# Decoding float64 weights in wider chunks, with the multiply on VectorE instead of GpSimd

## The chip, the cores and the metric

The kernel runs on one core of a Trainium2 chip. The metric is the device time of one execution in microseconds (us). TensorE (PE) does the matmuls, and PEld is its loading of weights; VectorE (DVE), ScalarE (ACT) and GpSimd (POOL) work on tiles in SBUF; SyncE (SP) issues most of the transfers. Each engine takes its own instructions strictly in the order in which the program gives them, and waits where an operand isn't ready or a buffer isn't free.

## The reference

Sigmoid attention is followed by an FFN with GELU. q, k and v are 8 x 12 x 448 x 64 (batches, heads, tokens, head size); the FFN has 3584 tokens, width 768 and hidden width 2048.

```python
scores = scale * np.matmul(q, k.transpose(0, 1, 3, 2)) - np.log(S)
attn = 1.0 / (1.0 + np.exp(-scores))
x = np.matmul(attn, v)          # heads side by side: 3584 x 768
h = x @ w_in                    # 768 x 2048
g = 0.5 * h * (1.0 + erf(h * inv_sqrt2))
out = g @ w_out                 # 2048 x 768
```

q, k and v are float32. The two weight matrices come in as float64, and the kernel gets them as 64-bit integers.

## The kernel before

**Splitting.** Matmuls run on float32 values in a rounded format, fp32r. Where more bits are wanted a value is split in two: ACT casts it to fp32r (the high part) and DVE subtracts that from the value (the low part). So `prepare_to` makes of every weight unit a tile `whl` with both parts (L236 on ACT, L237 on DVE), and `split_head` does the same for q and k of a head: `qs` (L291, L292) and `ka`, `kb` (cast L294, subtractions of 64 and 384 columns, L295 and L299).

**Decoding.** A chunk is 128 partitions by up to 384 weights, each with a low and a high 32-bit word. `start` takes the exponent bits `e` out of the high word with a mask (L124), shifts the mantissa `m` into place (L125) and joins bits of the low word to it (L128), all on DVE. `convert` makes a float32 power of two of `e` with two activations on ACT (L136, L139) and turns `m` from a signed integer into a float from 1 to 2 (L141 on DVE; for chunks 24 to 39 L145 on ACT). `end` joins the sign to `e` on DVE (L153), and GpSimd multiplies `m` by `e` (L162). The three steps are a pipeline: one step of the decoder runs `start` of chunk i, `convert` of chunk i-1 and `end` of chunk i-2, and then issues raw loads ahead of need on SP's queue (`load_to`, up to 8 raw buffers for the first 40 chunks). There are 32 chunks of `w_in` (16 units of 768) and 36 of `w_out` (12 units of 1024). A decoded unit is used from SBUF in the first pass over the tokens and stored to DRAM (L200) for the six passes after it.

**Order.** The order of all work is written out by hand. `attention_first` does the attention of batches 0 and 1, 24 heads one after the other. Per head `scores` does eight matmuls, the sigmoids on ACT and `split_head` for the head after the next; after every second head `values` does 16 matmuls for the pair, a cast on ACT (`xh`) and a subtraction on DVE (`xl`). Between `scores` and `values` stands `W.decode(n)`, which runs the decoder up to step n; PACE_A sets how many steps fall into this stage, PACE_F how many into `ffn1` of the first pass. Score and value tiles share four PSUM buffers, tag `pav`; the other score tile (`sc`, two key blocks) has one buffer.

Then come seven passes t of 512 token columns: `ffn1(t)`, 16 blocks of 18 matmuls with GELU behind each, and `window(t + 2, t)`, in which the 288 matmuls of `ffn2(t)` are cut into 24 parts and laid between the heads of the attention of batch t + 2. The last window has no attention left. Batches below 3 are "plain": their attention weights aren't split. In the first pass decoding goes on: one or two steps after each block of `ffn1`, three per head in `window`, until all chunks are done. In the first pass `prepare_to` in `ffn1` and `ffn2` splits a unit one or two units ahead of its matmuls, into two buffers `whl`.

Of the kernel before, what the change touches and what calls it, by code (L numbers as in the profile page):

```python
# [3 lines left out]

# [18 lines left out]
def tile_sigmoid_attention_gelu_ffn(  # L23
# [48 lines left out]


    PLAIN = 3
    RING = 3
    PACE_A, PACE_F = 20, 23
    SUB = 384
    RAW = (("raw", RING), ("a", 2)), (("raw", RING), ("a", 2), ("ah", 3))
    EARLY, AHEAD = PACE_A + PACE_F - 3, 4
    WST = 3  # L80
    SHIFT, KEPT = 1, 4
    AHD = 3
    MLO, MHI = 24, 40
# [7 lines left out]
    def decoder():  # L91


        chunks = [
            (kind, u, c0, min(SUB, width(kind) - c0))
            for kind, u in UNITS
            for c0 in range(0, width(kind), SUB)
        ]
        raws, parts, ended = {}, {}, [0]
        raw_ring = sb.tile([P, RING, 2 * SUB], U32, tag="raw", name="raw_ring", bufs=1)  # L100
        raw_next = itertools.cycle(range(RING))
        me_ring = sb.tile([P, RING, 2, SUB], U32, tag="me", name="me_ring", bufs=1)
        rings = [
            itertools.cycle([tag for n in range(4) for tag in ring if n < tag[1]]) for ring in RAW
        ]

        def load_to(n):
            for i in range(len(raws) + ended[0], min(n, len(chunks))):
                kind, u, c0, w = chunks[i]
                src = (w_in if kind == "in" else w_out)[u].rearrange("p a b -> p (a b)")  # L110
                tag, bufs = next(rings[i < EARLY])
                if tag == "raw":
                    raw = raw_ring[:, next(raw_next)]
                else:
                    raw = sb.tile([P, 2 * SUB], U32, tag=tag, name=f"raw{i}", bufs=bufs)
                raw = raw[:, : 2 * w]
                nc.sync.dma_start(raw.bitcast(I64), src[:, c0 : c0 + w])
                raws[i] = raw.rearrange("p (n t) -> p n t", t=2)

        def start(i):  # L120
            w = chunks[i][3]
            low, high = raws[i][:, :, 0], raws[i][:, :, 1]
            m, e = me_ring[:, i % RING, 0, :w], me_ring[:, i % RING, 1, :w]
            nc.vector.tensor_scalar(e, high, 0x7FF00000, None, op0=ALU.bitwise_and)  # L124
# [3 lines left out]
            nc.vector.scalar_tensor_tensor(  # L128
                m, low, 20, m, op0=ALU.logical_shift_right, op1=ALU.bitwise_or
            )  # L130
            parts[i] = m, e

        def convert(i):

            m, e = parts[i]
            nc.scalar.activation(  # L136
                e.bitcast(F32), e.bitcast(I32), AF.Relu, bias=1151.0 * 2**23, scale=-8.0
            )
            nc.scalar.activation(e, e.bitcast(F32), AF.Relu, bias=255.0 * 2**23, scale=-1.0)  # L139
            if not MLO <= i < MHI:  # L140
                nc.vector.tensor_scalar(  # L141
                    m.bitcast(F32), m.bitcast(I32), 2.0**-32, 1.5, op0=ALU.mult, op1=ALU.add
                )
            else:
                nc.scalar.activation(  # L145
                    m.bitcast(F32), m.bitcast(I32), AF.Identity, bias=1.5, scale=2.0**-32
                )

        def end(i):
            high = raws.pop(i)[:, :, 1]  # L150
            ended[0] += 1
# [10 lines left out]
            nc.gpsimd.tensor_tensor(t, m.bitcast(F32), e.bitcast(F32), op=ALU.mult)  # L162

        load_to(2)
        yield False
        for i in range(len(chunks) + 2):
            if i < len(chunks):
                start(i)
            if 0 <= i - 1 < len(chunks):
                convert(i - 1)  # L170
            if i > 1:
                end(i - 2)
            load_to(max(min(i + AHEAD + 1, EARLY), i + 2))
            yield i > 1 and chunks[i - 2][2] + chunks[i - 2][3] == width(chunks[i - 2][0])
# [109 lines left out]
    def split_head(b, h):  # L284
        b, h = there(b, h)
        if b >= B or h >= NH:
            return
        hp, j = divmod(h, 2)
        qr, kr = raws[b, hp]
        qs = sb.tile([P, S], F32R, tag="qs", name=f"qs{b}_{h}", bufs=3)  # L290
        nc.scalar.copy(qs[rows(j)], qr[rows(j)])  # L291
        nc.vector.tensor_tensor(qs[rows(1 - j)], qr[rows(j)], qs[rows(j)], op=ALU.subtract)  # L292
        ka = sb.tile([P, S + TAIL], F32R, tag="ka", name=f"ka{b}_{h}", bufs=3)
        nc.scalar.copy(ka[:, :S], kr[:, j])  # L294
        nc.vector.tensor_tensor(  # L295
            ka[:, S:], kr[:, j, S - TAIL :], ka[:, S - TAIL : S], op=ALU.subtract
        )
        kb = sb.tile([P, S - TAIL], F32R, tag="kb", name=f"kb{b}_{h}", bufs=3)
        nc.vector.tensor_tensor(  # L299
            kb, kr[:, j, : S - TAIL], ka[:, : S - TAIL], op=ALU.subtract  # L300
        )
        heads[b, h] = qs, ka, kb
        if j == 1 and b >= PLAIN:
            vr = raws[b, hp, "v"]
            vs = sb.tile([P, 2, 4, 2 * D], F32R, tag="vs", name=f"vs{b}_{hp}")
            nc.vector.tensor_copy(vs[:, :, :, :D], vr)
            nc.vector.tensor_tensor(vs[:, :, :, D:], vr, vs[:, :, :, :D], op=ALU.subtract)
            heads[b, hp, "v"] = vs

    def scores(b, h):  # L310
        plain = b < PLAIN
        qs, ka, kb = heads.pop((b, h))
        a = []
        for t in range(2):
            tag = ("al", ("wst", "wst", "ah")[b])[t] if plain else "a"
            bufs = {"wst": WST, "a": 2}.get(tag, 3)
            a.append(sb.tile([P, 2, S], F32, tag=tag, name=f"a{b}_{h}_{t}", bufs=bufs))
        last = ps_av.tile([P, 512], F32, tag="pav", name=f"sc{b}_{h}_l")[:, :S]
        sc0 = ps_av.tile([P, 512], F32, tag="pav", name=f"sc{b}_{h}_0")[:, :S]
        sc1 = ps_sc.tile([P, 2, 512], F32, tag="sc", name=f"sc{b}_{h}_1")[:, :, :S]  # L320
        if plain:
            nc.tensor.matmul(last[:D], ka[:, S - TAIL : S], qs, start=True, stop=False)
            nc.tensor.matmul(last[:D], ka[:, S:], qs, start=False, stop=True)
        else:

            nc.tensor.matmul(last, ka[:, S - TAIL :], qs, start=True, stop=True)  # L326
        for c in range(3):
            keys = slice(c * P, c * P + P)
            o = sc0 if c == 0 else sc1[:, c - 1]
            nc.tensor.matmul(o, ka[:, keys], qs, start=True, stop=False)  # L330
# [249 lines left out]
```

## Time and profile before

| | |
|---|---|
| median of 3 runs | 1288.09 us (1288.07 to 1288.74) |
| the profiled execution, its own time | 1286.42 us |
| its span, first to last instruction | 1284.7 us |
| PE busy | 1240.6 us (97%) |
| ACT busy | 872.5 us (68%) |
| DVE busy | 827.1 us (64%) |
| POOL busy | 89.2 us (7%) |

The profiled execution took 1.7 us longer than its span; the median of the runs is another 1.7 us higher. Matmuls are pipelined and their ends are modelled, so that the record of one lasts longer than the time by which it holds up the next: the distance of two starts is what PE needs. The same holds, by about 0.1 us, for neighbours on DVE and ACT. In a group line, the figures behind the bar are the busy time of the group in us and the mean duration of one instruction in ns, and behind the second bar the time for which the engine sat idle just before them, with what ended most of it. All of POOL's busy time lies in the first 300 us.

### The profile page before, as it was taken

What the parts mean: (1) busy time and instruction counts of PE and PEld (TensorE: products, weight loads), DVE (VectorE), ACT (ScalarE), POOL (GpSimd) and SP (SyncE); (2) the same over time, 40 slices, a digit from 0 to 9 for tenths busy, and PEclk for the clock granted to TensorE, in tenths of its full rate; (3) what the DMA queues carried; (4) which work ended last, traced back from release to release, by engine and by line L of the source; (5) the groups of instructions that cost most, each with busy time, mean ns of one, the idle gap of its engine ahead of it and who ended that gap; (6) DMA issues with size and microseconds to landing.
All of it is one profiled execution on the core that took longest, in us unless ns stands there. A gap on an engine that the chain in (4) does not pass through costs nothing.

```text
span 1284.7 us, 15676 instructions
## 1 busy us (share of the span) xinstructions
PE 1240.6 (97%) x5448; PEld 985.1 (77%) x5448; DVE 827.1 (64%) x1359; ACT 872.5 (68%) x1427; POOL 89.2 (7%) x84
## 2 busy tenths in 40 slices
PE   7888888999999999999999999999999999999998
PEld 4445665666888888888888888888888888888887
DVE  6776888883358873489734798436984358863420
ACT  8997777764459974499844898447995469964421
POOL 1112333440000000000000000000000000000000
PEclk9999998999999999999999999999999999999999
DMA  8664646652444314444234442244422444323331
GB/s 302 232 203 144 225 162 201 200 185 95 135 153 153 108 54 132 149 152 135 66 95 157 150 150 70 82 162 153 142 74 91 151 148 141 105 66 98 113 123 35
DMA packets 83775, 176.41 MB, mean 137 GB/s; under 512 B 24432, under 2 KB 37744, under 8 KB 83696
## 3 DMA queue, kind: packets, MB, share of 16 engines
q1 hardware_dynamic: 81968, 169.12, 40.6%
q0 software_dynamic: 1728, 6.29, 1.2%
q8 instruction: 43, 0.70, 0.2%
q14 instruction: 36, 0.29, 0.1%
HBM read 149.03 MB, written 26.35 MB: 137 GB/s over the span
## 4 chain that ended last, share of the span: by engine, by line
PE 82%; DVE 7%; ACT 5%; issue 2%; POOL 2%; DMA 2%; SPq 0%; DVEq 0%; POOLq 0%; ACTq 0%
PE po L496 11%; PE po L497 11%; PE po L498 11%; PE ph L449 11%; PE ph L451 11%; PE ph L450 11%; PE pav L397 7%; PE sc L330 4%; PE sc L331 4%; PE pav L363 2%; ACT a L354 2%; DVE whl L237 2%; POOL w_out L162 1%; DVE me_ring L153 1%; PE sc_l L326 1%
## 5 line engine op out<-in xcount | busy, mean ns | idle before, releaser
L449 PE MATMUL ph<-xh,whl 128*128 128x512 f32 x672 | 267.2, 398 | 10.6 <-DVE whl L237 10.6
L496 PE MATMUL po<-g,whl 128*128 128x512 f32 x672 | 264.1, 393 | 9.5 <-DVE whl L237 9.4
L450 PE MATMUL ph<-xl,whl 128*128 128x512 f32 x672 | 266.5, 397 | 0.0
L451 PE MATMUL ph<-xh,whl 128*128 128x512 f32 x672 | 266.3, 396 | 0.0
L497 PE MATMUL po<-g,whl 128*128 128x512 f32 x672 | 262.9, 391 | 0.0
L498 PE MATMUL po<-g,whl 128*128 128x512 f32 x672 | 262.8, 391 | 0.0
L237 DVE TENSOR_TENSOR whl<-wst,whl 128x768 fp32r<-128x768 f32 (+1 forms) x168 | 179.6, 1072 | 67.0 <-ACT whl L236 63.6
L466 DVE TENSOR_TENSOR g<-gf,g 128x512 fp32r<-128x512 f32 x112 | 77.8, 694 | 224.0 <-ACT g L465 224.0
L464 ACT ACTIVATE gf<-ph 128x512 f32<-128x512 f32 x112 | 66.9, 597 | 216.2 <-PE ph L451 201.5
L449 PEld LDWEIGHTS ph<-xh,whl 128*128 128x128 f32 x672 | 126.6, 188 | 44.7 <-DVE whl L237 13.7
L236 ACT CAST whl<-wst 128x768 fp32r<-128x768 f32 (+1 forms) x168 | 155.4, 928 | 2.2 <-PE po L498 0.8
L496 PEld LDWEIGHTS po<-g,whl 128*128 128x128 f32 x672 | 126.6, 188 | 39.0 <-DVE whl L237 11.8
L451 PEld LDWEIGHTS ph<-xh,whl 128*128 128x128 f32 x672 | 126.7, 188 | 30.7
L450 PEld LDWEIGHTS ph<-xl,whl 128*128 128x128 f32 x672 | 126.6, 188 | 30.3
L354 ACT ACTIVATE a<-sc 128x896 f32<-128x896 f32 x192 | 129.6, 727 | 27.8 <-PE sc L331 23.5
L498 PEld LDWEIGHTS po<-g,whl 128*128 128x128 f32 x672 | 126.6, 188 | 27.0
L497 PEld LDWEIGHTS po<-g,whl 128*128 128x128 f32 x672 | 126.6, 188 | 23.8
L330 PE MATMUL sc<-qs,ka 128*128 128x448 f32 x288 | 109.3, 379 | 13.2 <-ACT a L354 12.7
L347 DVE TENSOR_TENSOR al<-a,ah 128x896 fp32r<-128x896 f32 x120 | 97.8, 854 | 34.8 <-ACT ah L346 34.8
L331 PE MATMUL sc<-qs,kb 128*128 128x448 f32 x288 | 107.6, 374 | 0.0
L292 DVE TENSOR_TENSOR qs<-qr,qs 64x448 fp32r<-64x448 f32 x96 | 62.1, 646 | 45.1 <-ACT qs L291 43.3
L346 ACT CAST ah<-a 128x896 fp32r<-128x896 f32 x120 | 85.6, 753 | 6.1 <-PE pav L397 4.7
(62 smaller groups left out, 1514.1 us busy)
## 6 DMA issues: line engine op xcount, KB each, us to landing
wst<-scr_in SPq DMA_DIRECT2D x96, 384.0 KB, 3.0
wst<-scr_out SPq DMA_DIRECT2D x72, 512.0 KB, 3.2
kr<-k_dram SPq DMA_DIRECT2D x47, 448.0 KB, 4.5
vr<-v_dram SPq DMA_DIRECT2D x48, 256.0 KB, 4.1
qr<-q_dram SPq DMA_DIRECT2D x48, 224.0 KB, 3.2
out_dram<-ob SPq DMA_DIRECT2D x42, 224.0 KB, 2.0
raw<-w_in_dram SPq DMA_DIRECT2D x20, 384.0 KB, 4.6
scr_in<-w_in SPq DMA_DIRECT2D x16, 384.0 KB, 4.2
```

What stands on the lines that cost most here:

```text
L236: nc.scalar.copy(hl[:, 0, :w], t[:, :w])
L237: nc.vector.tensor_tensor(hl[:, 1, :w], t[:, :w], hl[:, 0, :w], op=ALU.subtract)
L330: nc.tensor.matmul(o, ka[:, keys], qs, start=True, stop=False)
L331: nc.tensor.matmul(o, kb[:, keys], qs, start=False, stop=True)
L347: nc.vector.tensor_tensor(al[t][:, c], a[t][:, c], ah[t][:, c], op=ALU.subtract)
L354: nc.scalar.activation(a, sc, AF.Sigmoid, bias=NEG_LOG_S, scale=SCALE)
L449: nc.tensor.matmul(ph, wl, xh[:, cc], start=cc == 0, stop=False)
L450: nc.tensor.matmul(ph, wh, xl[:, cc], start=False, stop=False)
L451: nc.tensor.matmul(ph, wh, xh[:, cc], start=False, stop=cc == NC - 1)
L496: nc.tensor.matmul(po, wl, g[fc][:, 0], start=first, stop=False)
L497: nc.tensor.matmul(po, wh, g[fc][:, 1], start=False, stop=False)
L498: nc.tensor.matmul(po, wh, g[fc][:, 0], start=False, stop=last)
```

## The change

Chunks are 768 wide for `w_in` and 512 for `w_out`: 16 and 24 of them instead of 32 and 36. The mantissa is kept as an unsigned integer with its leading one set (shift by 11, OR instead of XOR), so that conversion, scaling by 2^-31 and the product with `e` are one `scalar_tensor_tensor` on DVE. L141, L145 and the GpSimd multiply are gone; POOL still issues the stores of `w_out`. The decoder has two stages: a step runs `start` of chunk i, the two activations of the same chunk among it, and then `end` of chunk i-1. The raw words have three buffers, and chunk i+2 is loaded behind `end` of chunk i-1, whose buffer it takes. PACE_A and PACE_F are halved with the chunks; `window` has two steps per head instead of three, none directly behind `scores`.

In `split_head` the two k tiles become one, `ks`. For plain batches its low part is one subtraction of 448 columns, and for batches 0 and 1 the cast of k runs on DVE. `qs` and `ks` have two buffers instead of three. For batches from 3 on the two `a` tiles of a head are one tile of the same total size with one buffer. The matmuls stay the same in number and size.

```diff
-    PACE_A, PACE_F = 20, 23
-    SUB = 384
+    PACE_A, PACE_F = 10, 11
+    SUB_IN, SUB_OUT = NC * P, NFH * P // 2
...
+        def load(i):
...
+            if i % 3 < 2:
+                raw = raw_ring[:, i % 3]
+            else:
+                raw = sb.tile([P, 2 * SUB], U32, tag="a", name=f"raw{i}", bufs=1)
...
         def start(i):
...
             nc.vector.tensor_scalar(e, high, 0x7FF00000, None, op0=ALU.bitwise_and)
+
             nc.vector.tensor_scalar(
-                m, high, 12, 0x80000000, op0=ALU.logical_shift_left, op1=ALU.bitwise_xor
+                m, high, 11, 0x80000000, op0=ALU.logical_shift_left, op1=ALU.bitwise_or
             )
             nc.vector.scalar_tensor_tensor(
-                m, low, 20, m, op0=ALU.logical_shift_right, op1=ALU.bitwise_or
-            )
-            parts[i] = m, e
-
-        def convert(i):
-
-            m, e = parts[i]
+                m, low, 21, m, op0=ALU.logical_shift_right, op1=ALU.bitwise_or
+            )
+
             nc.scalar.activation(
                 e.bitcast(F32), e.bitcast(I32), AF.Relu, bias=1151.0 * 2**23, scale=-8.0
             )
             nc.scalar.activation(e, e.bitcast(F32), AF.Relu, bias=255.0 * 2**23, scale=-1.0)
-            if not MLO <= i < MHI:
-                nc.vector.tensor_scalar(
-                    m.bitcast(F32), m.bitcast(I32), 2.0**-32, 1.5, op0=ALU.mult, op1=ALU.add
-                )
-            else:
...
+            parts[i] = m, e
 
         def end(i):
...
-            nc.gpsimd.tensor_tensor(t, m.bitcast(F32), e.bitcast(F32), op=ALU.mult)
-
-        load_to(2)
+            nc.vector.scalar_tensor_tensor(
+                t, m, 2.0**-31, e.bitcast(F32), op0=ALU.mult, op1=ALU.mult
+            )
+
+        load(0)
+        load(1)
         yield False
-        for i in range(len(chunks) + 2):
+        for i in range(len(chunks) + 1):
+            if i == 0:
+                load(2)
             if i < len(chunks):
                 start(i)
-            if 0 <= i - 1 < len(chunks):
-                convert(i - 1)
-            if i > 1:
-                end(i - 2)
-            load_to(max(min(i + AHEAD + 1, EARLY), i + 2))
...
+            if i > 0:
+                end(i - 1)
+                load(i + 2)
...
+        ks = sb.tile([P, 2 * S], F32R, tag="ks", name=f"ks{b}_{h}")
+        if b < PLAIN:
+
+            (nc.vector.tensor_copy if b < 2 else nc.scalar.copy)(ks[:, :S], kr[:, j])
+            nc.vector.tensor_tensor(ks[:, S:], kr[:, j], ks[:, :S], op=ALU.subtract)
...
             scores(att, h)
-            if ffn == 0:
-                W.decode(PACE_A + PACE_F + 3 * h + 1 - SHIFT)
...
                 if ffn == 0:
-                    W.decode(PACE_A + PACE_F + 3 * h + 2 + part - SHIFT)
+                    W.decode(PACE_A + PACE_F + 2 * h + part + 1)
```

More of the change, by code (lines that the diff above doesn't have):

```diff
@@ L1 @@
-import itertools
 import math
@@ L74, in tile_sigmoid_attention_gelu_ffn @@
     PLAIN = 3
-    RING = 3
-    PACE_A, PACE_F = 20, 23
-    SUB = 384
[L78 to L83, printed above, removed]
+    PACE_A, PACE_F = 10, 11
+    SUB_IN, SUB_OUT = NC * P, NFH * P // 2
+    SUB = max(SUB_IN, SUB_OUT)
+    KEPT = 4
+    WST, AHD = 3, 3
     UNITS = [("in", u) for u in range(NF)] + [("out", u) for u in range(NO)]
@@ L94, in decoder @@
         chunks = [
-            (kind, u, c0, min(SUB, width(kind) - c0))
+            (kind, u, c0, sub)
             for kind, u in UNITS
-            for c0 in range(0, width(kind), SUB)
-        ]
[L99 to L113, printed above, removed]
-                else:
[L115 to L118, printed above, removed]
+            for sub in (SUB_IN if kind == "in" else SUB_OUT,)
+            for c0 in range(0, width(kind), sub)
+        ]
+        raws, parts = {}, {}
+        raw_ring = sb.tile([P, 2, 2 * SUB], U32, tag="raw", name="raw_ring", bufs=1)
+        me_ring = sb.tile([P, 2, 2, SUB], U32, tag="me", name="me_ring", bufs=1)
+        def load(i):
+            if i >= len(chunks):
+                return
+            kind, u, c0, w = chunks[i]
+            src = (w_in if kind == "in" else w_out)[u].rearrange("p a b -> p (a b)")
+            if i % 3 < 2:
+                raw = raw_ring[:, i % 3]
+            else:
+                raw = sb.tile([P, 2 * SUB], U32, tag="a", name=f"raw{i}", bufs=1)
+            raw = raw[:, : 2 * w]
+            nc.sync.dma_start(raw.bitcast(I64), src[:, c0 : c0 + w])
+            raws[i] = raw.rearrange("p (n t) -> p n t", t=2)
         def start(i):
@@ L122, in start @@
             low, high = raws[i][:, :, 0], raws[i][:, :, 1]
-            m, e = me_ring[:, i % RING, 0, :w], me_ring[:, i % RING, 1, :w]
+            m, e = me_ring[:, i % 2, 0, :w], me_ring[:, i % 2, 1, :w]
             nc.vector.tensor_scalar(e, high, 0x7FF00000, None, op0=ALU.bitwise_and)
             nc.vector.tensor_scalar(
-                m, high, 12, 0x80000000, op0=ALU.logical_shift_left, op1=ALU.bitwise_xor
+                m, high, 11, 0x80000000, op0=ALU.logical_shift_left, op1=ALU.bitwise_or
             )
             nc.vector.scalar_tensor_tensor(
-                m, low, 20, m, op0=ALU.logical_shift_right, op1=ALU.bitwise_or
+                m, low, 21, m, op0=ALU.logical_shift_right, op1=ALU.bitwise_or
             )
-            parts[i] = m, e
-        def convert(i):
-            m, e = parts[i]
             nc.scalar.activation(
@@ L161, in end @@
             t = first_w[kind, u][:, c0 : c0 + w]
-            nc.gpsimd.tensor_tensor(t, m.bitcast(F32), e.bitcast(F32), op=ALU.mult)
-        load_to(2)
+            nc.vector.scalar_tensor_tensor(
[3 more added lines that the diff above has]
+        load(1)
         yield False
-        for i in range(len(chunks) + 2):
+        for i in range(len(chunks) + 1):
+            if i == 0:
+                load(2)
             if i < len(chunks):
                 start(i)
-            if 0 <= i - 1 < len(chunks):
-                convert(i - 1)
-            if i > 1:
-                end(i - 2)
-            load_to(max(min(i + AHEAD + 1, EARLY), i + 2))
-            yield i > 1 and chunks[i - 2][2] + chunks[i - 2][3] == width(chunks[i - 2][0])
+            if i > 0:
+                end(i - 1)
+                load(i + 2)
+            yield i > 0 and chunks[i - 1][2] + chunks[i - 1][3] == width(chunks[i - 1][0])
     class Weights:
@@ L289, in split_head @@
         qr, kr = raws[b, hp]
-        qs = sb.tile([P, S], F32R, tag="qs", name=f"qs{b}_{h}", bufs=3)
+        qs = sb.tile([P, S], F32R, tag="qs", name=f"qs{b}_{h}")
         nc.scalar.copy(qs[rows(j)], qr[rows(j)])
         nc.vector.tensor_tensor(qs[rows(1 - j)], qr[rows(j)], qs[rows(j)], op=ALU.subtract)
[L293 to L302, printed above, removed]
+        ks = sb.tile([P, 2 * S], F32R, tag="ks", name=f"ks{b}_{h}")
+        if b < PLAIN:
+            (nc.vector.tensor_copy if b < 2 else nc.scalar.copy)(ks[:, :S], kr[:, j])
+            nc.vector.tensor_tensor(ks[:, S:], kr[:, j], ks[:, :S], op=ALU.subtract)
+        else:
+            c = S - TAIL
+            nc.scalar.copy(ks[:, :S], kr[:, j])
+            for to, n in (S, slice(c, S)), (S + TAIL, slice(0, c)):
+                low = ks[:, to : to + n.stop - n.start]
+                nc.vector.tensor_tensor(low, kr[:, j, n], ks[:, n], op=ALU.subtract)
+        heads[b, h] = qs, ks
         if j == 1 and b >= PLAIN:
@@ L311, in scores @@
         plain = b < PLAIN
[L312 to L317, printed above, removed]
+        qs, ks = heads.pop((b, h))
+        if plain:
+            a = []
+            for t in range(2):
+                tag = ("al", ("wst", "wst", "ah")[b])[t]
+                a.append(sb.tile([P, 2, S], F32, tag=tag, name=f"a{b}_{h}_{t}", bufs=3))
+        else:
+            at = sb.tile([P, 2, 2, S], F32, tag="a", name=f"a{b}_{h}", bufs=1)
+            a = [at[:, 0], at[:, 1]]
         last = ps_av.tile([P, 512], F32, tag="pav", name=f"sc{b}_{h}_l")[:, :S]
@@ L321, in scores @@
         if plain:
-            nc.tensor.matmul(last[:D], ka[:, S - TAIL : S], qs, start=True, stop=False)
-            nc.tensor.matmul(last[:D], ka[:, S:], qs, start=False, stop=True)
+            for n in range(2):
+                k_last = ks[:, (n + 1) * S - TAIL : (n + 1) * S]
+                nc.tensor.matmul(last[:D], k_last, qs, start=n == 0, stop=n == 1)
         else:
-            nc.tensor.matmul(last, ka[:, S - TAIL :], qs, start=True, stop=True)
+            nc.tensor.matmul(last, ks[:, S - TAIL : S + TAIL], qs, start=True, stop=True)
         for c in range(3):
-            keys = slice(c * P, c * P + P)
             o = sc0 if c == 0 else sc1[:, c - 1]
-            nc.tensor.matmul(o, ka[:, keys], qs, start=True, stop=False)
-            nc.tensor.matmul(o, kb[:, keys], qs, start=False, stop=True)
+            for n, lows in enumerate((0, S if plain else S + TAIL)):
+                keys = slice(lows + c * P, lows + c * P + P)
+                nc.tensor.matmul(o, ks[:, keys], qs, start=n == 0, stop=n == 1)
         tail = a[0][D:, 1]
```

4 lines of the change are left out of this document (removed).

## The prediction

> **What bounds the kernel now.** I read the busy time by stage first, then who PE waits for, then the timeline at those waits. PE's records give the stages (their start us; PE, PEld, DVE, ACT and POOL busy; granted clock; DMA): A is the attention of batches 0 and 1, B the first FFN half with decoding, C the window of batch 2 with the first `ffn2`, and then the rest.
> ```profile
> 4.60:109.50 104.90, 90.63 (x384) 46.35 (x384) 75.56 (x176) 92.36 (x167) 17.15 (x17) 0.97 0.70 237
> 109.50:190.86 81.36, 70.72 (x290) 54.75 (x289) 69.06 (x128) 57.99 (x111) 26.27 (x24) 0.98 0.56 182
> 190.86:313.64 122.78, 112.26 (x482) 77.35 (x480) 89.71 (x192) 78.59 (x139) 45.55 (x40) 0.96 0.52 169
> 313.64:1284.70 971.06, 967.00 (x4297) 806.64 (x4295) 591.99 (x863) 640.86 (x1007) 0.00 (x0) 1.00 0.37 119
> ```
> The reader is to see that PE is busy for 967 of the last 971 us at full clock, that no decoding is left there, and that only the first 313.64 us can move. What PE and DVE wait for there, up to 300 us (engine line, releaser: us, times, longest):
> ```profile
> PE sc L330 <- ACT a L354: 12.7, 10, 2.2
> PE ph L449 <- DVE whl L237: 10.6, 7, 2.0
> PE po L496 <- DVE whl L237: 9.4, 4, 3.7
> DVE me_ring L124 <- POOL w_out L162: 15.6, 16, 1.2
> ```
> PE's floor in each stage follows from the starts of its matmuls (start, duration):
> ```profile
> 110.09 0.40 PE L451 MATMUL ph<-xh,whl 128*128 128x512 f32 x1
> 110.32 0.40 PE L449 MATMUL ph<-xh,whl 128*128 128x512 f32 x1
> 29.72 3.38 PE L363 MATMUL pav<-a,vr 128*64 128x448 f32 x16
> 33.03 0.41 PE L322 MATMUL sc_l<-qs,ka 128*64 128x448 f32 x1
> 37.48 0.74 PE L330 MATMUL sc<-qs,ka 128*128 128x448 f32 x1 [2.15 <-ACT a L354]
> 36.00:40.00 4.00, 2.52 (x6) 1.82 (x6) 3.53 (x10) 3.87 (x8) 1.00 (x1) 0.65 0.46 169
> ```
> A 512-column matmul takes 0.233 us of PE, a 448-column one 3.31/16 = 0.207. A holds 384 of these (79 us), B 288 of the former (67 us), C 288 and 192 (107 us): the stages lie 25, 14 and 16 us above their floors. The last two rows show a stall of 2.15 us with the granted clock at 0.65 around it.
>
> In A, ACT is the bound. One head on ACT, by its starts: sigmoids, q cast, k cast, tail sigmoid, two exponent steps, next head.
> ```profile
> 53.83 1.35 ACT L354 ACTIVATE a<-sc 128x896 f32<-128x896 f32 x2
> 55.21 0.56 ACT L291 CAST qs<-qr 64x448 fp32r<-64x448 f32 x1
> 55.80 0.57 ACT L294 CAST ka<-kr 128x448 fp32r<-128x448 f32 x1
> 56.39 0.54 ACT L354 ACTIVATE a<-sc_l 64x448 f32<-64x448 f32 x1
> 56.95 0.52 ACT L136 ACTIVATE me_ring<-me_ring 128x384 f32<-128x384 int32 x1
> 57.50 0.53 ACT L139 ACTIVATE me_ring<-me_ring 128x384 uint32<-128x384 f32 x1
> 57.93 1.33 ACT L354 ACTIVATE a<-sc 128x896 f32<-128x896 f32 x2
> 35.66 0.51 ACT L372 CAST xh<-pav 128x448 fp32r<-128x448 f32 x1
> 8.66 1.24 ACT a L354 x2
> 104.92 1.26 ACT a L354 x2
> 2.12 5.04 DMA raw_ring<-w_in_dram
> ```
> That is 4.1 us; with `xh` in every second head, and less in heads without a chunk, the 23 heads from 8.66 to 104.92 average 4.19 us. The last row is the first raw load, which held the start until 7.16.
>
> **Prices** (mean ns behind the comma; means over the stage in which they stand):
> ```profile
> L128 DVE SCALAR_TENSOR_TENSOR me_ring<-raw,me_ring 128x384 uint32<-128x384 uint32 x12 | 6.7, 559 | 0.4
> L124 DVE TENSOR_SCALAR me_ring<-raw 128x384 uint32<-128x384 uint32 x12 | 4.3, 355 | 0.0
> L124 DVE TENSOR_SCALAR me_ring<-raw 128x256 uint32<-128x256 uint32 x4 | 1.2, 293 | 1.3 <-POOL w_out L162 1.2
> L136 ACT ACTIVATE me_ring<-me_ring 128x384 f32<-128x384 int32 x18 | 9.4, 524 | 1.9 <-DVE me_ring L124 1.5
> L136 ACT ACTIVATE me_ring<-me_ring 128x256 f32<-128x256 int32 x10 | 4.2, 417 | 18.7 <-DVE me_ring L124 18.7
> L406 DVE CAST xh<-x 128x448 fp32r<-128x448 f32 x30 | 11.8, 394 | 1.0
> L299 DVE TENSOR_TENSOR kb<-kr,ka 128x384 fp32r<-128x384 f32 x24 | 13.2, 552 | 0.0
> L466 DVE TENSOR_TENSOR g<-gf,g 128x512 fp32r<-128x512 f32 x15 | 10.6, 706 | 3.1 <-ACT g L465 3.1
> L237 DVE TENSOR_TENSOR whl<-wst,whl 128x768 fp32r<-128x768 f32 x96 | 91.9, 959 | 20.3 <-ACT whl L236 17.5
> L237 DVE TENSOR_TENSOR whl<-wst,whl 128x1024 fp32r<-128x1024 f32 x72 | 87.7, 1224 | 46.7 <-ACT whl L236 46.1
> L237 DVE TENSOR_TENSOR whl<-w_in,whl 128x768 fp32r<-128x768 f32 x14 | 23.1, 1647 | 0.0
> L295 DVE TENSOR_TENSOR ka<-kr,ka 128x64 fp32r<-128x64 f32 x24 | 5.4, 226 | 0.9 <-ACT ka L294 0.2
> L295 DVE TENSOR_TENSOR ka<-kr,ka 128x64 fp32r<-128x64 f32 x11 | 8.7, 793 | 0.2
> L236 ACT CAST whl<-w_out 128x1024 fp32r<-128x1024 f32 x11 | 11.5, 1045 | 0.0
> ```
> Two-tensor DVE work costs 1.04 ns an element (959 to 1224), so 559 becomes 0.96 us at 768 and 0.69 at 512, and L299's 552 becomes 0.62 at 448, for q's and k's low parts. TENSOR_SCALAR costs 0.48 ns an element (293 to 355): 0.54 and 0.42. An exponent step, 0.84 ns an element: 0.85 and 0.63. The new multiply isn't in the trace; it is a SCALAR_TENSOR_TENSOR with a conversion, and I take L128's price. A floor is that price less the 0.1 us by which neighbours overlap, a ceiling 1.65 us, the slowest two-tensor row. A chunk thus costs DVE 2x0.54+3x0.96 = 3.96 us (3.8 with overlaps) at 768, 2.9 at 512, one exponent pair on ACT 1.7 or 1.26.
>
> **Part by part.** GpSimd's multiply goes, with two things: DVE's waits for it (15.6 us), and the slowness of DVE beside it (1647 instead of 959 ns in B, and for 64 elements 793 in C instead of the 226 of A). Its fixed costs halve, and the conversion to float falls into the multiply.
>
> But the exponent steps now follow `start` of the same chunk, not of the one before. ACT is in order: its exponent step waits for DVE's mask, which stands behind DVE's q and k work of that head, and the next head's sigmoids stand behind it. DVE also does one chunk in one piece of 3.8 us, ahead of `xl`, which frees a PSUM tile.
>
> A. Per pair of heads without a chunk, PE's own loop is: values 3.31, scores of the odd head 8x0.207 = 1.65, the big sigmoid 0.9, half of the next scores 0.83, hand-overs 0.3: 7.0 us. ACT needs less: 4.1 without the k cast (0.59) and the exponent steps (0.98), twice, and `xh`: 5.6. After head i decoding goes to step 2+8(i+1)//24: the 7 chunks of the loop come every third head, 4 in even and 3 in odd ones. Times from here on count from the even head's first sigmoid. In an even head DVE's q and k work (0.62 + 0.39 + 0.62, overlapped 1.5) starts as the q cast ends, at 1.9; with 3.8 of chunk and `xl` behind it DVE is at 7.4. The next even head's first score tile, which takes the buffer that `xl` frees, would have started at 5.2. Of these 2.2 us PE's own wait for the odd head's sigmoid hides 0.4: 8.8 instead of 7.0. In an odd head the sigmoid starts at 5.0 (3.31+1.65) and the q cast ends at 6.9; q and k work and the mask take DVE to 8.9, the exponent pair ACT to 10.6, and only then come the next sigmoids, instead of at 7.5. The small one frees the tile for which PE would ask 1 us after 10.2, the end of the next values, and it comes at 12.0; with what is late behind it PE loses 2.0. Loop: 11.5x7.0 + 4x1.8 + 3x2.0 = 93.7, and as much for the slow clock as now (0.03 of 104.9 is 3.1): 96.8, against 96.3 from 8.66 to 104.92. The ends of the unknown: both waits hidden (-13) or the two added in full (+9). Start: two chunks of 768 are loaded and exponentiated ahead of the first sigmoid, not one of 384. Two more exponent pairs' worth is 4x0.85-2x0.53 = 2.3 us, the doubled load up to 5.04 more, partly beside each other; I take +3, from 1 to 6. A: +3.5. The k cast itself (0.59 off ACT, 0.39 on DVE) is inside the loops; one subtraction of 448 (0.62) replaces 0.55+0.23.
>
> B. DVE has 16x(0.71+0.96), 11 chunks (six at 768, one mixed, four at 512: 39 us) and two heads' q and k (2.5): 68 us, PE 67. Chunks come in runs of three iterations with 1 us of DVE too much in each; the loop lets about 1 us go, then PE waits: 3 us in all. B: 70 to 71 against 81.4, -11, from -5 (overlaps gone, ACT late behind the exponent) to -13.
>
> C. DVE's sum per head is 0.6+0.6+1.2+0.3+2x2.9 = 8.5, PE's 1.65 + 1.65 + 23.7x0.233 = 8.8. What decides is ACT and DVE in turn: sigmoids to tail 3.1, weight copy 1.05, DVE 1.22, mask 0.4, exponent beside the rest of the chunk 2.5, next mask 0.4, exponent 1.26: 9.6 with overlaps, 10.1 with `xh`. So 9.87 for the 10.5 heads with chunks (21 steps, 2 each; before 28, 3 each), 8.8 for the 1.5 others, 2.8 for the 12 matmuls kept for the end, less 3 by which PE may run ahead: 116.6 against 122.8. C: -6, from -13 (PE's floor plus 3) to +7 (11.1 a head).
>
> Costing nothing: the merged `ks` and `a` tiles and two q and k buffers instead of three, since ACT's sigmoid in front of `split_head` has already waited for the same matmuls; without that cover, one score group (1.65) per head in A. A raw load on SP now waits for the multiply's step in front of it, and q, k, v loads and the `scr_in` stores queue behind it; its data is needed two chunks on, at least 7 us in B (3.8 and the subtractions of two blocks, 3.3), against 5.04 for half its size at the start. If that fails, about 1 us a chunk in B.
>
> Sum: 3.5-11-6 = -13.5 on the profiled 1286.42 gives 1272.9; the median of the runs is 1.7 higher: 1274.6. A measurement tells apart about 0.2% (2.6 us).
>
> **Rivals.** (1) A gains as well, the waits hidden because ACT runs late anyway: A -7, B -13, C -13, total -33: 1255. For: ACT is the bound of A and is freed. Against: the 1.5 us behind DVE is new.
> (2) The clock. The row at 36.00 shows it at 0.65 around a 2.15 us stall, while most of the other nine waits left it alone. The forecast has 7 such stalls in A; if each costs some 1.7 us of slow matmuls, 7x1.7 less the 3.1 us lost already is +9: 1283.5. [...]
> (3) Slower: in C the first exponent step of an even head stands behind `xh`, which waits for PE's values, and the two engines take turns at 11.9 us a head: C 10.5x11.9+13 = 138, +15, total +7.5: 1295.6. It decides from 11.2 us a head. For it, ACT's waits for the mask in the first 300 us now:
> ```profile
> ACT me_ring L136 <- DVE me_ring L124: 43.7, 29, 3.1
> ```
> They are 43.7 us in spite of the stage between mask and exponent. Against: DVE's sum of 8.5 leaves it free time in every head.
> (4) The change doesn't do what it says: the 1647 ns aren't GpSimd's doing. B loses 16x0.69 = 11 of its gain, C 0.7x10: +4.5, 1292.6. Against: the 64-element row.
>
> **Numbers.** Forecast 0.58 (own range 1267 to 1283), rival 1 0.15, rival 2 0.11, rival 3 0.11, rival 4 0.05. Faster takes the forecast and the first two rivals but for their upper edges (0.05): 0.79; within 0.2% these edges and some of rival 4: 0.07; slower the rest: 0.14. The range 1257 to 1291 leaves out some 0.09 of rival 1 below, and 0.11 of rivals 3 and 4 above.
>
> **What would show it.** First sigmoid near 12 us; A about 104 to 109 us long with ACT idle ahead of the exponent step; the weight subtraction at 0.96 us in B and PE waits for it under 4 us; about 9.9 us per head in C; the rest at 971 us. Wrong: A shorter by over 5, C's heads over 10.4, or the last stage changed.

## The result, and the profile after

| | before | after |
|---|---|---|
| median | 1288.08 us (1288.03 to 1288.74, 4 runs) | 1295.24 us (1294.26 to 1296.25, 4 runs) |
| the profiled execution, its own time | 1286.42 us | 1296.25 us |
| its span | 1284.7 us | 1294.5 us |

The change makes the kernel slower by 7.2 us: the ratio is 1.0054, with a 95% interval from 1.0037 to 1.0072. The forecast was 1274.6 us, 13.5 us faster, with a range from 1257 to 1291. Sign and range were both wrong.

These are the stages of the changed kernel, as in the prediction's first fence (start and end; length; PE, PEld, DVE, ACT, POOL busy; granted clock; DMA share and rate). A begins here at 0. The fifth row is A from a start that answers to the 4.60 of before.
```profile
0.00:120.36 120.36, 95.19 (x384) 47.90 (x384) 79.35 (x129) 80.20 (x129) 0.20 (x4) 0.93 0.56 193
120.36:197.02 76.66, 71.00 (x290) 55.70 (x289) 62.45 (x88) 46.80 (x73) 0.67 (x1) 0.96 0.62 202
197.02:323.70 126.68, 113.75 (x481) 78.71 (x480) 88.06 (x144) 77.30 (x123) 5.84 (x11) 0.95 0.56 176
323.70:1294.50 970.80, 967.00 (x4297) 807.32 (x4295) 591.82 (x863) 640.26 (x1007) 0.00 (x0) 1.00 0.36 119
...
5.10:120.36 115.26, 95.19 (x384) 47.90 (x384) 78.21 (x126) 77.58 (x125) 0.00 (x0) 0.93 0.56 195
```
A ends at 120.36 instead of 109.50 (+10.9), B takes 76.66 instead of 81.36 (-4.7), C 126.68 instead of 122.78 (+3.9), and the rest is the same to 0.3 us. The fifth row is the one to dwell on: ACT was the bound of A, and its busy time fell from 92.4 to 77.6 us as the change has it. Yet the stage grew by 10. Less work on the bounding engine went along with a longer stage.

Who waits for whom shows what replaced the work. In these lines, up to 320 us, stand the total, the number of waits and the longest.
```profile
ACT me_ring L125 <- DVE me_ring L116: 66.8, 40, 5.4
PE sc L323 <- ACT a L346: 24.5, 14, 5.8
ACT g L457 <- DMA scr_in<-w_in: 4.7, 1, 4.7
```
There are 40 chunks and 40 waits of ACT for the mask: the exponent step of every chunk waits for DVE's first instruction of the same chunk (L116), 1.7 us on average. PE's wait for the sigmoids has doubled, from 12.7 us to 24.5. One such place in A, in the timeline of the changed kernel (start, duration, the idle time before in brackets):
```profile
76.20 0.55 DVE L116 TENSOR_SCALAR me_ring<-raw_ring 128x768 uint32<-128x768 uint32 x1
...
76.79 0.85 ACT L125 ACTIVATE me_ring<-me_ring 128x768 f32<-128x768 int32 x1 [1.68 <-DVE me_ring L116]
77.67 0.85 ACT L128 ACTIVATE me_ring<-me_ring 128x768 uint32<-128x768 f32 x1
78.42 0.51 ACT L364 CAST xh<-pav 128x448 fp32r<-128x448 f32 x1
78.83 1.35 ACT L346 ACTIVATE a<-sc 128x896 f32<-128x896 f32 x2
...
79.99 0.62 DVE L365 TENSOR_TENSOR xl<-pav,xh 128x448 fp32r<-128x448 f32 x1
...
53.02 2.31 PE L323 MATMUL sc<-qs,ks 128*128 128x448 f32 x6 [2.20 <-ACT a L346]
80.23 2.23 PE L323 MATMUL sc<-qs,ks 128*128 128x448 f32 x6 [2.20 <-ACT a L346]
107.47 2.17 PE L323 MATMUL sc<-qs,ks 128*128 128x448 f32 x6 [2.20 <-ACT a L346]
```
ACT stands idle for 1.68 us for the mask, does two exponent activations of 0.85, and only then the sigmoids for which PE waits 2.20 us. The subtraction `xl`, for which the prediction had PE wait in these even heads, is still running when PE starts again at 80.23, so it isn't what PE waited for. The three PE rows stand 27.2 us apart, which is six heads: two chunks fall on every six heads and meet them in the same way each time. The clock follows, in stretches of 3.41 us, the length of the drop:
```profile
77.29:80.71 3.42, 1.22 (x6) 0.71 (x5) 3.29 (x4) 3.36 (x7) 0.00 (x0) 1.00 0.20 50
80.71:84.12 3.41, 3.41 (x11) 1.73 (x12) 1.64 (x3) 2.09 (x5) 0.00 (x0) 0.50 0.99 312
84.12:87.53 3.41, 3.41 (x19) 1.41 (x16) 1.93 (x4) 1.39 (x3) 0.00 (x0) 1.00 0.98 359
```
Behind the stall PE does 11 matmuls in 3.41 us instead of 19.

### The profile page after: what moved, and what is told of

Same layout as the page of the kernel before. It is cut to its first block, busy times and chain, and to the rows that moved or that the text cites. A ratio compares the mean times of both kernels' runs of the same rounds, so it can differ in the third digit from the quotient of the medians.

```text
span 1294.5 us, 15251 instructions
## 1 busy us (share of the span) xinstructions
PE 1246.9 (96%) x5448; PEld 989.6 (76%) x5448; DVE 821.7 (63%) x1223; ACT 844.6 (65%) x1331; POOL 6.7 (1%) x16
## 4 chain that ended last, share of the span: by engine, by line
PE 82%; ACT 8%; DVE 6%; issue 2%; DMA 1%; SPq 0%; DVEq 0%; ACTq 0%
PE ph L441 11%; PE ph L442 11%; PE ph L443 11%; PE po L489 11%; PE po L488 11%; PE po L490 10%; PE sc L323 7%; PE pav L389 7%; ACT a L346 3%; PE pav L355 2%; DVE whl L221 1%; DVE me_ring L116 1%; ACT me_ring L125 1%; ACT whl L220 1%; PE sc_l L318 1%
## 5 line engine op out<-in xcount | busy, mean ns | idle before, releaser
L458 DVE TENSOR_TENSOR g<-gf,g 128x512 fp32r<-128x512 f32 x112 | 77.6, 693 | 233.3 <-ACT g L457 233.3
L221 DVE TENSOR_TENSOR whl<-wst,whl 128x768 fp32r<-128x768 f32 (+1 forms) x168 | 179.6, 1072 | 66.8 <-ACT whl L220 63.5
L323 PE MATMUL sc<-qs,ks 128*128 128x448 f32 x576 | 141.7, 382 | 25.0 <-ACT a L346 24.5
L323 PEld LDWEIGHTS sc<-qs,ks 128*128 128x128 f32 x576 | 111.3, 196 | 43.2 <-ACT a L346 30.7
L276 DVE TENSOR_TENSOR qs<-qr,qs 64x448 fp32r<-64x448 f32 x96 | 59.5, 620 | 50.6 <-ACT qs L275 48.2
```

The lines of the kernel that those rows point to most:

```text
L221: nc.vector.tensor_tensor(hl[:, 1, :w], t[:, :w], hl[:, 0, :w], op=ALU.subtract)
L323: nc.tensor.matmul(o, ks[:, keys], qs, start=n == 0, stop=n == 1)
```

## The experiments

Two theories were tried against each other. Theory 1: the loss sits in places where instructions stand in a wrong order (the exponent behind its own mask, the start, the stores of `w_in`, chunks pulled forward at the end of C). Theory 2: the work is the bound, above all DVE's, which has the multiply now, and moving waits moves nothing.

**Three places by themselves.** The first kernel decodes no chunk ahead of the pace: `prepare_to` asks for units ahead only once all are decoded.
```diff
-                self.load_to(i + WST if i + WST >= len(UNITS) else 0)
+                if self.decoded == len(UNITS):
+                    self.load_to(i + WST if i + WST >= len(UNITS) else 0)
```


> The changed kernel, but splitting a unit in the first window no longer pulls all chunks that are left forward. Theory 1 (the loss sits in four separate places: the start, the scr_in stores at the seam of A and B, these chunks pulled forward in C, and the exponent steps that wait for the mask): PE's stall of 5.8 us near 292 us and the slow clock behind it go, C falls from 126.7 to about 120, the time from 1295.2 to about 1289. Theory 2 (VectorE and ScalarE simply have too much decoding, and a wait taken away at one place comes back at the next): C stays at 125 or more, the time at 1294 to 1296.

It took 1288.83 us, ratio to before 1.0007 (0.9997 to 1.0016): 6.4 us of the loss are gone, and they lie in C.
```profile
196.27:316.51 120.24, 111.57 (x481) 76.89 (x480) 87.88 (x144) 77.12 (x123) 5.84 (x11) 0.97 0.59 186
```
In the changed kernel, unit 25 asks for the last units while four steps of the decoder are still to do, so they run in one go ahead of the next sigmoids, and ACT waits 1.63, 1.55 and 2.27 us for the masks of the last three. PE and its clock in the changed kernel at that place:
```profile
297.92 2.61 PE L323 MATMUL sc<-qs,ks 128*128 128x448 f32 x6 [5.78 <-ACT a L346]
...
294.00:298.00 4.00, 0.08 (x1) 0.08 (x1) 3.45 (x7) 3.04 (x6) 0.52 (x1) 0.72 0.64 252
298.00:302.00 4.00, 4.00 (x10) 3.39 (x11) 3.60 (x5) 3.90 (x7) 0.53 (x1) 0.50 0.33 131
```

The second puts the first three stores of `w_in` ahead of the last step of A.
```diff
+        W.store_to(3)
         W.decode(PACE_A)
```


> The changed kernel, but the first three scr_in stores are issued ahead of the last decoder step of the attention stage, so that they no longer queue behind a raw load. Theory 1: the GELU's wait for a store (4.7 us) and PE's stall of 3.9 us go, B falls from 76.7 to about 72, the time to about 1291. Theory 2: VectorE is the bound of B, the stall moves to a later block, the time stays within 1 us of 1295.

It took 1289.0 us, ratio 1.0007 (0.9997 to 1.0016), and B shrinks to what the prediction had for it:
```profile
120.05:189.96 69.91, 68.14 (x290) 53.76 (x289) 62.27 (x88) 46.85 (x73) 0.67 (x1) 1.00 0.64 205
```
What it removes is this chain in the changed kernel: SP's queue first holds a raw load that waits for its buffer, then the stores, whose source a later GELU overwrites, and then PE waits.
```profile
124.52 0.33 SPq L109 DMA_DIRECT2D raw<-w_in_dram  x1
124.90 3.08 SPq L184 DMA_DIRECT2D scr_in<-w_in  x4
...
130.57 0.60 ACT L457 ACTIVATE g<-ph 128x512 fp32r<-128x512 f32 x1 [4.74 <-DMA scr_in<-w_in]
...
132.94 0.79 PE L441 MATMUL ph<-xh,whl 128*128 128x512 f32 x1 [3.91 <-DVE whl L221]
```
Before, three of these stores were issued at 103.19.

The third drops the two chunks that are decoded ahead of the first head.
```diff
         load_v(0, 0)
-        W.decode(2)
         load_v(0, 1)
```


> The changed kernel, but the first two chunks are decoded behind the scores of head 0 instead of ahead of them. Theory 1: the first sigmoid starts at 8 us instead of 13.5, A gets shorter by 3 to 5 us (part comes back as the second head's sigmoid waits), the time is about 1291. Theory 2: ScalarE has the same work, A shorter by less than 1 us.

It took 1296.86 us, ratio 1.007 (1.0055 to 1.0085): nothing gained, against theory 1. The first sigmoid comes at 8.66 instead of 13.52, but the two exponent pairs, 3.4 us of ACT, now stand between the sigmoids of head 0 and those of head 1, and PE waits there:
```profile
18.29 1.86 PE L323 MATMUL sc<-qs,ks 128*128 128x448 f32 x4 [4.14 <-ACT a L346]
```
A ends at 120.65. So the late start is no loss by itself: the two exponent pairs cost A about as much at either place.

**The place of the exponent.** Here the two activations of chunk i are issued at the beginning of the next step, ahead of `start` of chunk i+1. Work, chunk sizes and paces stay.
```diff
         def start(i):
...
-            nc.scalar.activation(
-                e.bitcast(F32), e.bitcast(I32), AF.Relu, bias=1151.0 * 2**23, scale=-8.0
-            )
-            nc.scalar.activation(e, e.bitcast(F32), AF.Relu, bias=255.0 * 2**23, scale=-1.0)
...
+        def exponent(i):
+            e = parts[i][1]
+            nc.scalar.activation(
+                e.bitcast(F32), e.bitcast(I32), AF.Relu, bias=1151.0 * 2**23, scale=-8.0
+            )
+            nc.scalar.activation(e, e.bitcast(F32), AF.Relu, bias=255.0 * 2**23, scale=-1.0)
...
+            if i > 0:
+                exponent(i - 1)
             if i < len(chunks):
                 start(i)
```


> The changed kernel, but the two exponent steps of a chunk are issued one decoder step later, ahead of the next chunk's first VectorE instruction, so that ScalarE doesn't wait for the mask. Theory 1: ScalarE's waits for the mask fall from 66.8 us to below 20; in A the odd heads' stall (1.3 us, 3 times) goes, the even heads' stall of 2.2 us stays since it is the xl behind a whole chunk on VectorE; C's pairs of heads fall from 20.4 to 18 to 19 us; the time is 1286 to 1290. Theory 2: VectorE waits for the exponent in its stead, the time stays within 2 us of 1295.

It took 1271.03 us, ratio 0.987 (0.9851 to 0.9888): 24 us less than the changed kernel, where the expectation had 5 to 9. Its stages A, B, C, its waits and its stalls in A:
```profile
0.00:110.37 110.37, 90.42 (x384) 46.33 (x384) 79.22 (x129) 78.87 (x127) 0.20 (x4) 1.00 0.61 211
110.37:185.93 75.56, 69.94 (x291) 54.88 (x290) 62.44 (x88) 48.52 (x75) 0.67 (x1) 0.98 0.63 205
185.93:298.15 112.22, 108.64 (x482) 77.20 (x481) 86.96 (x144) 76.97 (x123) 5.85 (x11) 0.98 0.63 199
...
ACT me_ring L128 <- DVE me_ring L116: 13.6, 11, 5.4
...
51.08 1.49 PE L327 MATMUL sc<-qs,ks 128*128 128x448 f32 x6 [1.04 <-ACT a L350]
75.08 1.49 PE L327 MATMUL sc<-qs,ks 128*128 128x448 f32 x6 [1.04 <-ACT a L350]
```
ACT's wait for the mask falls from 66.8 to 13.6 us, six heads take 24.0 us instead of 27.2, the stall of 2.20 us is one of 1.04, and in the loop the clock stays at 1.00. The expectation had left that stall in place, as a wait for `xl`; it was one for the exponent. The listed 1.00 is no guide to the start of A: at 17.30 six matmuls take 2.44 us, at 24.23 they take 1.40, and the trace of the kernel with all three edits (below) has the same 2.44 at 17.38 under a listed 0.50. DVE is as busy in A as before the edit (79.2 against 79.35 us), so its work wasn't the bound there.

The counter-test does the same to the kernel before: `convert` of a chunk (the two activations and the conversion of the mantissa) directly behind its own `start`, all else as it was.
```diff
-            if 0 <= i - 1 < len(chunks):
-                convert(i - 1)
+            if i < len(chunks):
+                convert(i)
```


> The kernel before with one part of the change alone: the conversion stage is issued right behind the start of the same chunk, not one step later; GpSimd still multiplies. Theory 1: ScalarE's waits for the mask rise from 44 us to about 70; A gets longer by 8 to 12 us (ScalarE is A's bound and each of 18 chunks adds some 0.5 us behind VectorE's q and k work), C by 3 to 10; about 1300. Theory 2: no change beyond 2 us, since VectorE's sum is the same.

It took 1317.84 us, ratio 1.0238 (1.0223 to 1.0253). That is 30 us slower, from moving one call by a step, and more than theory 1 had put on it. A ends at 121.12, B takes 87.76 and C 134.19 us, and the waits for the mask rise from 43.7 us (29 times, first 300 us) to (first 343 us)
```profile
ACT me_ring L136 <- DVE me_ring L124: 82.3, 68, 2.2
```

**Is it the wait, or the exponent's place on ACT?** Putting the exponent a step later also changes its place among the sigmoids. So one kernel leaves ACT's order as the change has it and moves only DVE's mask: the one of chunk i+1 stands at the end of step i, behind the multiply of chunk i-1.
```diff
         def start(i):
...
-            nc.vector.tensor_scalar(e, high, 0x7FF00000, None, op0=ALU.bitwise_and)
...
+        def mask(i):
...
+            nc.vector.tensor_scalar(e, high, 0x7FF00000, None, op0=ALU.bitwise_and)
...
             if i > 0:
                 end(i - 1)
+            if i + 1 < len(chunks):
+                mask(i + 1)
```


> The changed kernel with one DVE instruction moved: the mask of chunk i+1 stands at the end of step i, behind the multiply of chunk i-1, so that the exponent step of a chunk no longer waits for a mask of its own step. ACT's order and all work stay as they are. Theory 1 (the loss is the wait for the mask, with what stands behind it on ACT): ACT's wait for the mask falls from 66.8 us to under 25, A from 120.4 to 110 to 113 without slow clock, C from 126.7 to 113 to 117, and the time from 1295 to 1271 to 1277. Rival (the exponent's own place on ACT, ahead of the next sigmoids, was the loss, and putting it a step later helped by moving it away from them): the mask wait falls, but the sigmoids come as late as now, and the time stays over 1288.

It took 1282.12 us, ratio 0.996 (0.9946 to 0.9974), between the two. In A the theory of the wait holds: A ends at 111.17, and ACT's wait for the mask there falls from 17.8 us to 4.8; the clock is 1.00 from 24 us on. C shrank by 3.7 us only, where 10 to 14 were expected. A and C, and one of the waits in C:
```profile
0.00:111.17 111.17, 89.77 (x384) 46.10 (x384) 80.50 (x130) 80.65 (x129) 0.20 (x4) 0.95 0.62 209
...
186.61:309.57 122.96, 111.70 (x481) 77.94 (x480) 88.25 (x143) 75.03 (x121) 6.20 (x11) 0.96 0.57 181
...
228.16 0.63 ACT L124 ACTIVATE me_ring<-me_ring 128x512 f32<-128x512 int32 x1 [2.95 <-DVE me_ring L133]
```
A head of C has two steps, one directly behind the other. There the mask for the second stands behind the whole first step on DVE, and each second exponent still waits some 3 us (28.1 us over C, of 32.0 in the changed kernel). The expectation had overlooked that. So in A it is the wait and not the place. In C nearly all of the wait was left, so this run doesn't part the two there; an earlier mask helps as far as something else lies between it and its exponent.

**The multiply alone.** This is the kernel before with the unsigned mantissa and the product on DVE, by which the conversions L141 and L145 fall away, and nothing else: 384-wide chunks, three steps, the k cast on ACT.
```diff
-                m, high, 12, 0x80000000, op0=ALU.logical_shift_left, op1=ALU.bitwise_xor
+                m, high, 11, 0x80000000, op0=ALU.logical_shift_left, op1=ALU.bitwise_or
...
-            nc.gpsimd.tensor_tensor(t, m.bitcast(F32), e.bitcast(F32), op=ALU.mult)
+            nc.vector.scalar_tensor_tensor(
+                t, m, 2.0**-31, e.bitcast(F32), op0=ALU.mult, op1=ALU.mult
+            )
```


> The kernel before with one part of the change alone: unsigned mantissa and the multiply on VectorE, nothing on GpSimd; chunks of 384, the three decoder stages and the k cast stay as before. Theory 1: the multiply's move is a gain by itself, since it takes GpSimd's slowing of VectorE away and the wait for the exponent isn't added: weight subtraction in B 0.96 instead of 1.65 us, B 81.3 to about 71, C 122.8 to 112 to 115, A within 2 us of 109.5; about 1268. Theory 2: the multiply on VectorE (0.55 us a chunk in place of the 0.35 us conversion) is what costs: A and C longer than before, 1288 to 1295.

It took 1269.4 us, ratio 0.9864 (0.985 to 0.9879). The fused multiply is worth some 18 us. They lie in B (74.35 us instead of 81.36) and C (110.33 instead of 122.78); A is 3 us longer, where 2 at most were expected. What the change adds to it (wider chunks, two stages, the k cast, the queue) takes some 25 us back.

**The k cast.** The changed kernel with the k cast of batches 0 and 1 on ACT again:
```diff
-            (nc.vector.tensor_copy if b < 2 else nc.scalar.copy)(ks[:, :S], kr[:, j])
+            nc.scalar.copy(ks[:, :S], kr[:, j])
```


> The changed kernel with the k cast back on ScalarE for batches 0 and 1. Theory 1: in A ScalarE gets 24 casts of 0.57 us (13.6 us) back, but VectorE's mask comes 0.39 us sooner, and the wait for it takes up some of it; A longer by 2 to 8 us, 1297 to 1303. Theory 2: VectorE is the bound of A, so that taking 0.39 us a head off it makes A shorter by 3 to 9 us, 1286 to 1292.

It took 1291.83 us, ratio 1.0039 (1.0025 to 1.0052). The changed kernel has 1.0054 (1.0037 to 1.0072), so the two can't be told apart; the 2 to 8 us that theory 1, with ACT as the bound of A, had added did not come, and A ends at 119.12. The same edit was made to the best version (below), where ACT no longer waits:

> The best version so far (exponent a step later, stores of w_in earlier, no chunks pulled forward) with the k cast of batches 0 and 1 back on ACT. In the changed kernel the same move cost nothing and even gained 3 us, since ACT stood waiting. Theory 1 (ACT waits only because of the mask; without that wait it is again the engine that bounds A, 4.1 us a head with 0.6 for the k cast): A grows from 110.7 to 113 to 118, the time from 1260 to 1262 to 1268. Rival (DVE bounds A, with 79 us of work in A against 80 on ACT): A shrinks by 2 to 6, the time falls to 1254 to 1258.

This time it took 1263.69 us, ratio 0.9808 (0.9791 to 0.9826), against 0.9792 (0.9775 to 0.9808) without the edit. That is 2 to 3 us more, with intervals that overlap; in the one profile of each, A ends at 113.18 instead of 110.73. The rival's 1254 to 1258 is out. In the changed kernel ACT has idle time ahead of each mask, and with 0.39 us a head less on DVE its wait for the mask in A falls from 17.8 us to 7.2, which takes up most of the 0.57 us a head added on ACT. Without the wait, ACT is the tighter one again, as far as differences this near to the noise can show it.

**The clock.** The version with the exponent a step later has a listed clock of 1.00 all through A, which its matmuls bear out from 24 us on. Stalls go into it: at heads 5, 9, 13 and 17 the big sigmoid is repeated once, twice, three and four times.
```diff
         sigmoid(a[1], sc1)
+        for _ in range({5: 1, 9: 2, 13: 3, 17: 4}.get(NH * b + h, 0)):
+            sigmoid(a[1], sc1)
```


> The version with the exponent a step later, whose granted clock is 1.00 all through A with stalls of PE up to 1.6 us. At four heads of A (5, 9, 13 and 17) the big sigmoid is repeated 1, 2, 3 and 4 times, which holds its score tile, and PE behind it, 1.2 us longer for each. Theory 1 (the slow clock follows the length of a stall): no drop behind the first, a drop to about 0.5 for some 3 us behind those whose PE wait is over 2 us, the second to the fourth; the whole is longer by the added waits, some 11 us, plus 1.5 us for each drop. [...]

One run took 1284.04 us; A ends at 121.91. PE's rows at the first, the second and the fourth place, and stretches of 3.41 us at all four (behind the comma PE's busy time; the clock is the third figure from the end):
```profile
34.12 1.08 PE L327 MATMUL sc<-qs,ks 128*128 128x448 f32 x4 [1.15 <-ACT a L352]
...
52.75 1.55 PE L327 MATMUL sc<-qs,ks 128*128 128x448 f32 x6 [3.20 <-DVE xl L371]
...
93.77 1.08 PE L327 MATMUL sc<-qs,ks 128*128 128x448 f32 x4 [4.00 <-ACT a L352]
...
33.56:36.97 3.41, 2.85 (x14) 1.44 (x16) 1.78 (x4) 3.33 (x6) 0.00 (x0) 1.00 0.28 88
...
50.63:54.04 3.41, 1.29 (x6) 1.05 (x6) 2.98 (x5) 2.78 (x5) 0.00 (x0) 1.00 0.53 94
54.04:57.45 3.41, 3.41 (x11) 1.19 (x12) 1.76 (x5) 2.45 (x4) 0.00 (x0) 0.50 1.00 362
...
67.69:71.11 3.42, 1.55 (x7) 0.61 (x5) 2.94 (x5) 3.09 (x5) 0.00 (x0) 1.00 0.75 242
71.11:74.52 3.41, 3.09 (x8) 1.46 (x8) 1.49 (x3) 2.89 (x5) 0.00 (x0) 0.50 0.93 306
...
88.17:91.59 3.42, 1.61 (x8) 1.04 (x7) 0.27 (x1) 2.52 (x3) 0.00 (x0) 1.00 0.18 67
91.59:95.00 3.41, 1.23 (x6) 0.87 (x8) 0.22 (x1) 3.32 (x6) 0.00 (x0) 1.00 0.00 0
95.00:98.41 3.41, 3.41 (x11) 0.98 (x8) 3.31 (x7) 3.35 (x6) 0.00 (x0) 0.50 0.00 0
```
Behind the stall of 1.15 us there is no drop, and behind those of 3.20 and 4.00 us there is one of 3.41 us each. At the third place no wait was over 2 us: 1.56 us for `ks`, then 0.18 and 0.32. Still the clock falls there at 71.1, for 6.8 us, and before the repeated sigmoids hold PE at 71.96. The drops in the loop stand at the stalls and nowhere else, the last one with the DMA engines idle, so the stalls set them off; but the length of one wait, theory 1's measure, isn't what decides.

**All mended.** The exponent a step later, the stores of `w_in` early and no chunks pulled forward, in one kernel:

> The changed kernel with three edits together: exponent steps one decoder step later, the first scr_in stores ahead of the last decoder step of the attention stage, and no chunks pulled forward in the first window. Theory 1, now with the exponent's place as the main cause: the parts add up where they lie in different stages: A 110, B 70 (store), C 112 or a little less (the pulled chunks cost less once ScalarE doesn't wait), 1271.0 less 5.5: 1265. Theory 2 (VectorE's and ScalarE's work is the bound, waits only move): B and C stay within 1 us of the kernel with the exponent edit alone, 1270 to 1271.

It took 1260.46 us, ratio 0.9792 (0.9775 to 0.9808): faster than both theories had it, and 27 us faster than before. Its stages A, B, C (the 0.95 of A lies ahead of 24 us):
```profile
0.00:110.73 110.73, 89.80 (x385) 46.11 (x385) 79.31 (x129) 78.92 (x127) 0.20 (x4) 0.95 0.66 221
110.73:180.47 69.74, 68.14 (x290) 53.76 (x289) 62.26 (x88) 48.48 (x75) 0.67 (x1) 1.00 0.64 204
180.47:288.75 108.28, 106.77 (x481) 76.05 (x480) 86.81 (x144) 76.66 (x123) 5.85 (x11) 1.00 0.66 207
```
B and C lie 3 and 1 us above the floors of 67 and 107 that the prediction worked out; A ends 1.2 us later than before. The multiply alone took 1269.4 us, so with the three places mended the rest of the change gives 9 us more; which part of it does isn't shown.

## Why the prediction was wrong

The forecast for the profiled execution was -13.5 us, and +9.8 came. Of the 23.3 us between them 7.4 lie in A, 6.3 in B and 9.9 in C, less 0.3 in the rest.

**The price of the instructions was right.** The multiply, which no trace had shown, was put at 0.96 us, and the weight subtraction of B back to 0.96 once GpSimd is quiet. Both came so, and rival 4 falls (changed kernel, groups of DVE in B):
```profile
L221 DVE TENSOR_TENSOR whl<-w_in,whl 128x768 fp32r<-128x768 f32 x14 | 13.4, 956 | 0.2
...
L143 DVE SCALAR_TENSOR_TENSOR w_in<-me_ring 128x768 f32<-128x768 uint32 x8 | 7.7, 958 | 0.3
```

**A: forecast +3.5, measured +10.9.** The start had +3, and took 4.9 (first sigmoid at 13.52 instead of 8.66). The loop, from the first big sigmoid to the last, had 93.7 + 3.1 = 96.8 us and took 102.1 (13.52 to 115.66).

Two steps failed here. One is "as much for the slow clock as now": the forecast had put seven stalls of 1.8 to 2.0 us into A, beside a row that showed a drop at 2.15 us, and kept the 3.1 us of two drops. Three came, at 1.56 us each (27.21 us for six heads with a drop, 25.65 for those from 27.37 to 53.02 without one): 4.7 us. The other is the length of a pair of heads: 25.65 us stands against 3x7.0 + 1.8 + 2.0 = 24.8, which over three such periods is 2.6 us. The 1.1 us left over lie outside these periods and weren't taken apart. In the four even heads the cause was wrong as well: the forecast had PE wait for `xl` behind the chunk on DVE, and PE waited for the sigmoids behind the exponent. That its 1.8 us is near the 2.20 measured is luck.

The mean clock of A, 0.93 against 0.97, makes the clock's share look larger: two fifths of the low time lie between 12.44 and 19.27, ahead of the loop's rhythm. Rival 2, which added 9 us of slow clock to the forecast's 3.5, was right in kind, and near A's size by luck, since the drops took 1.6 us more than the forecast had, not 9; no row of the prediction shows the 1.7 us of slow matmuls that it put on each stall, and what came in the loop were three drops at 1.56 us each and none at the fourth stall of 2.2 us. On B and C it failed like the forecast.

**B: forecast -11, measured -4.7.** The failed step stands under "costing nothing": that the stores of `w_in` queue behind a raw load on SP without harm. The price of a failure was given as about 1 us a chunk; what came was one place, 6.75 us, at the seam of A and B: a stall of 3.91 us, and behind it matmuls at 0.43 us each instead of 0.23. With the stores issued earlier B takes 69.91 us, at the edge of the forecast of 70 to 71.

**C: forecast -6, measured +3.9.** Two terms. Two of PE's waits for the split weights in the changed kernel, four heads apart, show the length of a head with chunks:
```profile
216.92 0.54 PE L488 MATMUL po<-g,whl 128*128 128x512 f32 x1 [2.71 <-DVE whl L221]
...
257.72 0.49 PE L488 MATMUL po<-g,whl 128*128 128x512 f32 x1 [2.04 <-DVE whl L221]
```
Four heads take 40.8 us, so one takes 10.2 instead of 9.87, which over 10.5 heads is 3.5 us. The other term is absent from the forecast: the chunks pulled forward at the end, 6.4 us. The diff leaves that line of `prepare_to` as it was; what is new is that the decoder isn't done when it is reached, and that its steps wait. Rival 3, on whose side the result lies, had 11.9 us a head and +15 us in C, and failed as a mechanism; that its 1295.6 us stands beside the measured 1295.24 is luck.

**The common root was named and underpriced.** "The exponent steps now follow `start` of the same chunk" was in the prediction, and its effect was followed head by head. What wasn't done was to price that edit by itself, against leaving it out: it is worth 24 us in the changed kernel and 30 in the one before. Set against that, the forecast's sum held gains of 13.5 us net.

The profiled executions agree with this: 10.9 - 4.7 + 3.9 - 0.3 is 9.8, the difference of the spans. The medians differ by 7.2 us only, since the profiled execution of before lay 1.7 us below its median and that of the changed kernel 1.0 above.

## What to carry to other kernels

When two in-order engines hand a value back and forth, each hand-over needs other work between producer and consumer on both: folding two pipeline steps into one cost a wait per item here (40 waits for 40 chunks, 66.8 us), and the waits fall on whatever stands behind in the queue. Price such a step by itself, in both orders, before summing it up with the gains, and price a queue entry by what stands behind it, at the seams of stages too. Stalls of TensorE brought slow matmuls with them here: the clock fell to 0.50 at three of the four stalls of 2.20 or 2.21 us in the changed kernel's loop, for some 1.6 us each, and at two of the five of 2.15 or 2.16 us in the kernel before. A forecast with such stalls should have that loss as a term of its sum.

## What the hardware showed that was not expected

The granted clock fell to 0.50 at stalls of 2.2 us, but not at every one. Of the four in the loop of A in the changed kernel, those at 53.02, 80.23 and 107.47 were followed by a drop, and the one of 2.21 at 27.37 wasn't. In the kernel before there are five of 2.15 or 2.16 us, with a drop at two (37.48 and 71.59), where the prediction had seen one. The drops of the changed kernel's loop lasted 3.41 us and cost about 1.6 us each.

So the length of a stall alone doesn't decide it; what else does isn't settled here. Nor are all drops of one length: up to 330 us, those of the changed kernel that begin at 12.44, 131.91 and 295.74 last 6.83 us, and those at 53.40, 80.71, 108.01, 217.24 and 258.20 last 3.41.
